# Attention scores of pairs 6 and 7 from two products of rounded operands in place of one float32 product, in a fused attention and feed-forward kernel with a written-out issue order

## The chip, the core and the metric

The kernel runs on one core of a Trainium2 chip. The metric is the device time of one execution in microseconds (us). Five engines work side by side: TensorE (PE, with its weight loads shown apart as PEld), VectorE (DVE), ScalarE (ACT), GpSimd (POOL) and the queue of SyncE (SP), from which nearly all DMAs are issued in order. A difference of 0.3%, some 3.1 us here, is about what a measurement of this kernel can tell from no change.

## What is computed

```
q, k, v: 8 batches x 8 heads x 576 x 64 float32;  f: 8 x 8 x 576
scores = q k^T / 8 + cum[i] - cum[j],  cum = cumsum(log(clip(f)));  causal
attn   = softmax(scores);   x = attn v            (4608 tokens x 512)
h = x w_in (512 x 2048);    out = (h cos h) w_out  (2048 x 512)
```

## The kernel before, in words

**Units.** The attention is cut into 32 pairs of heads (pair n belongs to batch n // 4), the feed-forward part into 16 units of tokens (unit u is one half of a batch, 320 or 256 tokens). A pair has two heads. Per head the causal scores are made in three groups of row blocks, one PSUM tile each: block 4 (two products of 288 columns), blocks 3 and 0 (448 and 64 columns), blocks 2 and 1 (320 and 192 columns). After a product, DVE adds the mask and finds the row extreme (line 879, 705 for pairs 0 to 3), ACT makes exp and the row sum (884, 715), POOL and DVE the reciprocal of the sum (889, 892), and ACT and DVE write the normalized weights as a high and a low float16 half (901, 905); a DMA transposes them (910) and PE multiplies them with v (934).

**Three kinds of scores.** `N32` and `NQ` set which pairs take which way. Pairs below `N32` = 4 are float32 throughout (`attention32`, scores in line 697, transposes on PE in line 668). Pairs from `N32` up to `NQ` = 8 load q and k as float32 (`load32`: one 288 KB load in line 636 and two loads of one row of the running sum in line 640 per head) and make the scores in one float32 product of 66 rows (line 865; the trace has each as two records). Pairs from `NQ` on run `prep` per head: a 576 KB load of q and k, laid out twice over 128 partitions (line 800), one rounding of all 1152 columns (line 801 on ACT or 802 on POOL), a DMA that copies rounded rows from tile to tile (803), two loads of rows of the running sum (806), and two subtractions that leave the rest after rounding (808 and 809, each on DVE or POOL). Their scores are two products of rounded operands that add up in PSUM (lines 867 and 868).

**Shared tiles.** The four q/k tiles of the float32 pairs are taken over by the two sets of the rounded pairs. At pair `NQ` an operation on POOL (`make`, line 787) clears each set (lines 369 to 371 and 791); it may start when the float32 pairs are done with those two tiles.

**The issue order.** Every operation is recorded with its engine and what it reads and writes, and `ORDER`, a table of numbers, says in which order the operations are issued; each engine runs its own in that order. A letter `a` behind a number takes the other engine (POOL for a rounding, a subtraction or a split). `+m` puts m filler products in front of a PE operation (line 1077: a constant tile times a constant mask of 448 columns, into the tile that the operation is about to overwrite). They compute nothing that is used.

```
N32, NQ, NACT = 4, 8, 1                                             # 44
gens = [(attention32 if n < N32 else attention)(n) ...]
if n < NQ: xb, q32 = load32(n, hd)                                  # attention
else: prep(hd); xb, q32 = list(SB[sets[hd]].values()), None
if q32: T.matmul(c, q32[0:66, 0, isl], q32[0:66, 1, d], ...)        # 865
else:                                                               # 867, 868
    T.matmul(c, hi[:, 0, isl], hi[:, 1, d], start=True, stop=False)
    T.matmul(c, co[0:68, 0, isl], co[0:68, 1, d], start=False, stop=True)
for _ in range(pads): T.matmul(fill(), ones, mask[:, 0:PAD], ...)   # 1077
```

The feed-forward part is `gemm1` (lines 964 to 994) and `gemm2` (1010 to 1019), with twelve float16 products to an operation. The weights are read as 64-bit words, converted, bounded and split at the start (lines 483 to 519), beside the pairs of batch 0.

Of the kernel before, what the change touches and what calls it, by code (L numbers as in the profile page):

```python
# [43 lines left out]
N32, NQ, NACT = 4, 8, 1  # L44
# [8 lines left out]
0 50 60 55 70 25 1 2 4 51 27 52 26 72 61 71 53 62 54 63 3 65 11 56 192 57 95 64 100 6 58 125 7a 170 33+44 28 34 35 40+1 66 37 29 36 67 12  # L53
85+1 41 59 68 78+1 30 175 86 124 96 69 73+1 191 87 42 9 79 44 123 31+1 97 185 38+2 155 215 80 101 156 245 157 74 190 158+3 39 98 81 13 171
32 159 43 176 172 45+2 177 10 48 160 178 75 161 15 311 173 82 131+6 312 162 102 47 163 88 126+1 89 186 46 132 116 138+1 149 174 187 164 180
127 83 24 93 150 216 84 139 179 205+4 133 140 49 217 430 135 243 188 14 90+8 218 1439 16 206 244 94 110 17 207 18 76+1 134 165 19a 92 181
198 128 117 182 91 20 193 199 189 183 141 425 115 166 21 431 200 184 167 77 435 432 142 310 275 22 219 433 276 5 23 146 277a 194 251+1 147
# [14 lines left out]
796 586a 786 601 604 813 787 597 797 818 542 799 617 605 798 819 602 773 598 800 820 618+1 801 607 814 802 606 949 821 619 803 948 825 804  # L72
620 774 621 599 822 837 805 622 826 623 608 624 806 658 600 625 807 641 662+1 827 626 828 838 659 642 808 678 627 839 643 609 676+1 823 628
679 644 663 629 664+2 809 677 630 645 810 829 631 646 811 830 660 840 831 632 832 610 672 665 661 633 841 877+1 634 673 647 674+1 878 635
648a 824 833 611 834 858+3 933 836 842 636 714 879 843 637 859 649 692 638 844 835 650 675 845 639 698 612 893 651 984 860 640 865 652 693
666 880 861 862 667 613 699 653 846 614 668 694 654 700 847 848 655 669 863 889 657 670 680 681 715 986 710 947 656 682 864 695 881 866 1438
701 867 683 868 882 869 696 883 895 870 671a 871 884 697 885 926 712 872 886 873 887 684 874 849 1148 890 876 875 896 702 902 853 891 927
914 897 903 850 716 898 711 1022 851 945 904 915 713 899 726 916 905 888 717 906 718 917 730 727 907 728 731 985 908 918 719 1026 900 919
1029 854a 969 909 703 920 901 729 724 910 921 911 922 720 913 912 950 970 923 686 685a 951 924 971 972 957 1027a 704 958 925 959 952 721 687
973 953 725 954 974 1031 960 955 975 732 1021 994 961 928 956 962 1082 963 733 964 965 976 987 966 977 734 995 1083 968 1032 978 705 996 967  # L80
979 997 735 941 929 1006 998 980 1445 999 688 1007 1023 1008 1000 988 1009 689 1010 1229 989 1028 1001 706 690 1011 990 1002 1012 691 991
1013 1003 1030 1014 946 1273 722 707 1015 992 723a 1004 1016 942 981 993 1017 736 934 943 737 1230a 1084 982 708 983 709 1085 1234a 1231
1033 1005 1018 1034 935 936a 1235 1040 1019 1086 1020 1052 1041 937 1068 1274a 1053 938 1054 1042 1055 1278a 1275 1070 1035 1276 1956 1043
1232 1036 1037 1069 939 1072 940 1056 1038 1071 1044 1074 1073 1045 1446 1046 1024 1057 1058 1279 1124 1314 1075 1047 1277 1076 1233 1270
1077 1126 1125 1048 1059 1039 1078 1122 1957 1025 1064 1049 1127 1060 1120 1061 1065 1050 1079 1243 1121 1062 1123 1236 1271 1128 1140 1080
1066 1129 1255 1100 1318 1315 1081 1051 1130 1134 1320a 1237 1238 1131 1101 1102 1244 1132 1087 1239 1319a 1256 1317 1245 1240 1103 1063
1257 1141 1246 1133a 1241 1287 1258 1138 1242 1259 1316 1288 1104 1247 1289 1280 1248 1290 1260 1249 1136 1250 1281 1135 1251 1291 1252 1139
# [1020 lines left out]
```

## Time and profile before

| | |
|---|---|
| Runs | 1042.11, 1043.04, 1045.21 us; median 1043.04 |
| The profiled execution's own time | 1040.97 us |
| Its span, first to last instruction | 1039.0 us |
| Busy, share of the span | PE 99%, PEld 80%, DVE 75%, ACT 76%, POOL 28% |
| Granted TensorE clock over the span | 1.00 of full speed |
| DMA | 144.77 MB, mean 139 GB/s |

The profiled execution stands 2.07 us under the median of the runs, and 1.97 us of its own time lie outside the span. PE's busy time counts a matmul from its start to its modelled end, so neighbours overlap; what one costs the engine is the distance from its start to the start of what follows.

### The profile page before, as it was taken

The numbers are of one execution on the slowest core, as the hardware profiler recorded it, in microseconds if no ns is written. First come the engines' busy times: TensorE is split into PE (matmuls) and PEld (weight loads), VectorE is DVE, ScalarE is ACT, GpSimd is POOL, SyncE is SP. The second block draws the span as 40 slices with busy tenths as digits, with TensorE's granted clock in tenths as the row PEclk, the third lists the DMA queues.
The fourth block names the chain that finished last, engine by engine and source line by source line (L and its number), as shares of the span: only waits on it lengthen the run. The fifth ranks groups of instructions, "written<-read, shape, count | busy, mean of one in ns | idle before, by whom it ended". The sixth has DMA issues, their size and how long they took to land. (4 is left out here: it accounts for less than half of the span.)

```text
span 1039.0 us, 23384 instructions
## 1 busy us (share of the span) xinstructions
PE 1027.0 (99%) x8915; PEld 831.6 (80%) x8916; DVE 774.9 (75%) x1710; ACT 789.5 (76%) x1711; POOL 294.8 (28%) x381
## 2 busy tenths in 40 slices
PE   8999999999999999999999999999999999999998
PEld 4788777778888877888778877888778877888787
DVE  8999998778678676787877688586877967663531
ACT  5999999788768797898877789686878877753431
POOL 3223213432341343332332424233141313300110
PEclk9999999999999999999999999999999999999999
DMA  8997525856685757668465766947466583520001
GB/s 261 288 321 200 130 55 128 185 107 162 154 175 147 163 132 163 139 144 183 114 145 135 176 142 159 193 83 164 124 170 136 121 189 56 122 39 16 7 14 34
DMA packets 255920, 144.77 MB, mean 139 GB/s; under 512 B 223736, under 2 KB 231928, under 8 KB 255808
## 3 DMA queue, kind: packets, MB, share of 16 engines
q1 hardware_dynamic: 255680, 143.27, 58.4%
q8 instruction: 70, 1.15, 0.4%
q14 instruction: 42, 0.34, 0.1%
q10 hardware_dynamic: 128, 0.01, 0.0%
HBM read 71.41 MB, written 9.68 MB: 78 GB/s over the span
## 5 line engine op out<-in xcount | busy, mean ns | idle before, releaser
L1010 PE MATMUL hp<-g,W2s 128*128 128x320 f16 (+1 forms) x3072 | 391.8, 286 | 0.2
L964 PE MATMUL hp<-xh,W1s 128*128 128x320 f16 (+1 forms) x2048 | 381.3, 286 | 1.5 <-ACT h L970 1.4
L964 PEld LDWEIGHTS <-W1s 128*128 128x128 f16 x3072 | 295.5, 98 | 78.6 <-issue 1.8
L1010 PEld LDWEIGHTS <-W2s 128*128 128x128 f16 x3072 | 296.3, 98 | 76.1 <-issue 0.6
L964 PE MATMUL hp<-xl,W1s 128*128 128x256 f16 (+1 forms) x1024 | 292.6, 286 | 0.0
L905 DVE SCALAR_TENSOR_TENSOR PS<-pa,ri,PS 128x576 f16<-128x576 f32 (+3 forms) x280 | 146.1, 544 | 57.3 <-ACT PS L901 55.9
L884 ACT ACTIVATE pa<-pa,nb 128x576 f32<-128x576 f32 (+4 forms) x280 | 141.5, 506 | 48.5 <-DVE nb L879 43.1
L901 ACT ACTIVATE PS<-pa,ri 128x576 f16<-128x576 f32 (+3 forms) x280 | 137.7, 531 | 31.1 <-DVE ri L892 27.0
L889 POOL TENSOR_SCALAR ri<-L 128x1 f32<-128x1 f32 (+1 forms) x168 | 53.9, 321 | 352.0 <-ACT pa L884 347.1
L879 DVE CUSTOM_DVE_ANT_0 pa<-pa,mask 128x576 f32<-128x576 f32 (+4 forms) x280 | 134.7, 500 | 24.0 <-PE pa L868 20.4
L970 ACT ACTIVATE h<-hp 128x320 f32<-128x320 f32 (+1 forms) x256 | 100.1, 411 | 36.5 <-PE hp L964 32.8
L994 POOL TENSOR_TENSOR g<-h,g 128x1024 f16<-128x1024 f32 (+1 forms) x32 | 83.5, 2609 | 149.0 <-ACT g L992 147.3
L985 DVE TENSOR_TENSOR h<-h,r 128x1280 f32<-128x1280 f32 (+1 forms) x64 | 89.6, 1399 | 34.4 <-ACT r L983 33.9
L983 ACT ACTIVATE r<-r,halfpi,m_inv 128x1280 f32<-128x1280 f32 (+1 forms) x64 | 86.2, 1348 | 31.2 <-DVE r L981 29.0
L981 DVE SCALAR_TENSOR_TENSOR r<-r,m_b,h 128x1280 f32<-128x1280 int32 (+1 forms) x64 | 93.6, 1462 | 1.1
L867 PE MATMUL pa<-Q 128*128 128x288 f32 (+4 forms) x288 | 90.4, 327 | 1.2 <-DVE PS L905 0.7
L979 DVE TENSOR_SCALAR r<-h,m_a 128x1280 int32<-128x1280 f32 (+1 forms) x64 | 54.9, 858 | 44.9 <-ACT h L970 43.0
L992 ACT CAST g<-h 128x1280 f16<-128x1280 f32 (+1 forms) x64 | 73.8, 1154 | 10.6 <-DVE h L985 10.4
L934 PEld LDWEIGHTS <-vv 128*64 128x64 f16 x1512 | 68.6, 110 | 10.3 <-issue 9.5
L868 PE MATMUL pa<-Q 68*128 68x288 f32 (+4 forms) x288 | 76.6, 304 | 0.0
L934 PE MATMUL pa<-pt,vv 128*64 128x256 f16 (+2 forms) x1512 | 76.6, 254 | 0.0
L1016 ACT ACTIVATE ot<-hp,m_o 128x320 f32<-128x320 f32 (+1 forms) x64 | 32.2, 503 | 47.6 <-PE hp L1010 36.2
(127 smaller groups left out, 1182.5 us busy)
## 6 DMA issues: line engine op xcount, KB each, us to landing
stage<-in_dram SPq DMA_DIRECT2D x48, 576.0 KB
stage<-in_dram SPq DMA_DIRECT2D x32, 320.0 KB
v<-in_dram SPq DMA_DIRECT2D x32, 320.0 KB
h<-in_dram SPq DMA_DIRECT2D x16, 512.0 KB
g<-in_dram SPq DMA_DIRECT2D x16, 512.0 KB
Q<-Q SPq DMA_DIRECT2D x48, 144.0 KB
out_dram<-ot SPq DMA_DIRECT2D x32, 160.0 KB
Q<-in_dram SPq DMA_DIRECT2D x16, 288.0 KB
```

Source lines behind the costliest of these rows:

```text
L867: T.matmul(c, hi[:, 0, isl], hi[:, 1, d], start=True, stop=False)
L879: op("DVE", c_dve(w) + 0.008, lambda view=view, ib=ib, o=o, w=w, mk=mk, c=c: V.tensor_tensor_reduce(out=view(ib, o, w), in0=view(ib, o, w) ...
L884: op("ACT", c_act(w, True, 2), lambda view=view, ib=ib, o=o, w=w, c=c: A.activation(view(ib, o, w), view(ib, o, w), AF.Exp, bias=nb.get()[ ...
L901: op("ACT", c_act(w, True, 1), lambda view=view, ib=ib, o=o, w=w, c=c, out_=out_: A.activation(out_(0), view(ib, o, w), AF.Copy, scale=ri. ...
L905: op("DVE", c_dve(w) + 0.06, lambda view=view, ib=ib, o=o, w=w, c=c, out_=out_: V.scalar_tensor_tensor(out_(1), view(ib, o, w), ri.get()[: ...
L934: T.matmul(d, vv.get()[:, jb, hd, kv], m, start=first and x == 0, stop=last and x == 2)
L964: T.matmul(hp.get()[:, 0:w_], WS_[1][:, at(1, 4 * c + cb), w, fs], x.get(), start=(n == 0), stop=(n == 11))
L970: op("ACT", c_act(w_, True), lambda hp=hp, k=k: A.activation(h.get()[:, k, 0:w_], hp.get()[:, 0:w_], AF.Copy, scale=float(2.0 ** -24)), re ...
L981: op("DVE", c_dve(N) + 0.045, lambda: V.scalar_tensor_tensor(fl(r), fl(r).bitcast(I32), b1.get()[:, c:c + 1], fl(h), op0=ALU.mult, op1=ALU ...
L983: op("ACT", c_act(N, aps=2), lambda: A.activation(fl(r), fl(r), AF.Sin, scale=inv.get()[:, c:c + 1], bias=halfpi), reads=[inv], writes=[r] ...
L985: op("DVE", c_dve(N), lambda: V.tensor_tensor(fl(h), fl(h), fl(r), op=ALU.mult), reads=[r], writes=hk, prio=pr)
L1010: T.matmul(po.get()[:, 0:w_], WS_[2][:, at(2, 4 * c + k), w, msl], gh.get()[:, i, k, 0:w_], start=(n == 0), stop=(n == 47))
```

## The change

One constant changes, `NQ` from 8 to 6, and the whole of `ORDER` (4,299 operations before, 4,315 after).

```diff
-N32, NQ, NACT = 4, 8, 1
+N32, NQ, NACT = 4, 6, 1
 ...
 ORDER = """
-0 50 60 55 70 25 1 2 4 51 27 52 26 72 61 71 53 62 54 63 3 65 11 56 192 57 95 64 100 6 58 125 7a 170 33+44 28 34 35 40+1 66 37 29 36 67 12
 ...
```

The table's rows tell a reader nothing; what it does is counted from the two tables. Pairs 6 and 7 go over from `load32` to `prep`. Filler products: 44 in front of the first score product before, 36 now; behind it 55 before, 83 now. Of these 55 and 83 lie 39 and 56 in front of PE operations of pairs 0 to 3 or of the scaling of the weights and of v, 16 and 27 further on. The four roundings of pairs 6 and 7 are one on POOL and three on ACT, their eight subtractions five on DVE and three on POOL. Over the whole program ACT has 9 roundings more and POOL 5 fewer, DVE 2 subtractions fewer and POOL 10 more. POOL has 2 fewer of the splits of the weights and 2 fewer of v, DVE as many more. The number of changes between the exp and the sine tables on ACT is the same.

PE at the start of the program; `pa` and `hp` are PSUM tiles, PS the staging tile of the softmax, L1077 a filler. Before, the rows behind the 44 fillers:

```order
L697 MATMUL pa_166<-Q 128x448
L697 MATMUL pa_166<-Q 128x64
L697 MATMUL pa_213<-Q 128x288 x2
L1077 LDWEIGHTS ones
L1077 MATMUL pa_219<-mask,ones 128x448
L697 MATMUL pa_219<-Q 128x320
L697 MATMUL pa_219<-Q 128x192
L1077 LDWEIGHTS ones
L1077 MATMUL pa_231<-mask,ones 128x448
L697 MATMUL pa_231<-Q 128x320
L697 MATMUL pa_231<-Q 128x192
```

Of the change, behind its 36 fillers:

```order
L697 MATMUL pa_160<-Q 128x448
L697 MATMUL pa_160<-Q 128x64
L697 MATMUL pa_202<-Q 128x288 x2
L697 MATMUL pa_209<-Q 128x320
L697 MATMUL pa_209<-Q 128x192
L1077 LDWEIGHTS ones
L1077 MATMUL pa_218<-mask,ones 128x448
L697 MATMUL pa_218<-Q 128x320
L697 MATMUL pa_218<-Q 128x192
L668 MATMUL hp<-eyef,PS_81 128x128 x4
```

The first head's three groups now stand together, behind eight fillers fewer, and the first transposes follow the second head's first group.

PE at the first score group of pair 6 (L964 is `gemm1` of unit 1). Before:

```order
L964 MATMUL hp<-xl_1637,W1s 128x256
L1077 LDWEIGHTS ones
L1077 MATMUL pa_1858<-mask,ones 128x448
L865 MATMUL pa_1858<-Q 128x320
L865 MATMUL pa_1858<-Q 128x192
L1077 LDWEIGHTS ones
L1077 MATMUL hp<-mask,ones 128x448
L964 LDWEIGHTS W1s
```

Now:

```order
L964 MATMUL hp<-xl_1578,W1s 128x256
L867 MATMUL pa_1893<-Q 128x320
L868 MATMUL pa_1893<-Q 128x320
L867 MATMUL pa_1893<-Q 128x192
L868 MATMUL pa_1893<-Q 128x192
L1077 LDWEIGHTS ones
L1077 MATMUL hp<-mask,ones 128x448
```

Two float32 products became four of rounded operands, and both fillers stand behind the group.

The SP queue at the operands of pair 6 (v, Q, stage: the loads of v, the q/k tiles, the loads of q and k and of v; pt: transposed softmax weights). Before:

```order
L640 DMA Q<-cum_d 1x576
L636 DMA Q<-in_dram 64x2x576
L910 DMA_TRANSPOSE pt_2024<-PS_82 128x12x128
L640 DMA Q<-cum_d 1x576
L636 DMA Q<-in_dram 64x2x576
L1019 DMA out_dram<-ot 128x320
```

Now:

```order
L910 DMA_TRANSPOSE pt_1520<-PS_82 128x12x128
L803 DMA Q<-Q 64x576
L910 DMA_TRANSPOSE pt_1718<-PS_81 128x18x128
L806 DMA Q<-cum_d 2x576
L582 DMA stage<-in_dram 128x640
L806 DMA Q<-cum_d 2x576
L800 DMA stage<-in_dram 128x1152
```

The copy of the rounded rows and the two row loads of pair 6's first head stand between transposes, where a load from memory and one-row loads stood.

## Rows read from the trace of the kernel before

**Rows 1.** The page: busy time of each engine, its share of the span and its instructions; and the granted TensorE clock in 40 equal slices of the span, in tenths (9 is 0.9 or more).
```profile
PE 1027.0 (99%) x8915; PEld 831.6 (80%) x8916; DVE 774.9 (75%) x1710; ACT 789.5 (76%) x1711; POOL 294.8 (28%) x381
...
PEclk9999999999999999999999999999999999999999
```

**Rows 2.** The table of windows: from and to in us of the span, length, busy time of each engine (with its instructions), granted clock, DMA share and GB/s.
```profile
0.00:13.00 13.00, 10.71 (x45) 5.22 (x46) 9.80 (x17) 4.79 (x8) 6.42 (x24) 1.00 0.74 224
13.00:60.00 47.00, 44.27 (x278) 34.21 (x277) 44.64 (x129) 39.83 (x119) 10.51 (x20) 1.00 0.97 292
60.00:100.00 40.00, 39.62 (x290) 34.20 (x289) 39.42 (x120) 38.24 (x112) 12.36 (x28) 1.00 0.87 258
100.00:143.00 43.00, 42.65 (x344) 32.28 (x343) 42.04 (x92) 40.79 (x89) 7.98 (x13) 1.00 0.46 105
143.00:206.00 63.00, 62.58 (x529) 48.29 (x529) 52.95 (x118) 55.48 (x113) 22.84 (x32) 1.00 0.62 141
206.00:1039.00 833.00, 827.20 (x7442) 677.41 (x7436) 586.01 (x1240) 610.38 (x1274) 234.69 (x267) 1.00 0.56 125
```

**Rows 3.** The same windows for the fillers of line 1077 alone: length, PE and PEld with their counts.
```profile
13.00:60.00 47.00, 10.32 (x39) 3.93 (x39) 1.00 0.97 292
...
206.00:1039.00 833.00, 0.00 (x0) 0.00 (x0) 1.00 0.56 125
```

**Rows 4.** The chain of work that ended last, in order of time: start in us, us, engine, tile, line, how many.
```profile
951.61 19.91 PE hp L964 x156
...
1001.59 34.01 PE hp L1010 x288
```

**Rows 5.** The waits of PE over the whole span, longest first: who waited for whom, us in total, times, longest.
```profile
PE pa L1077 <- POOL ones L346: 2.3, 1, 2.3
PE hp L964 <- ACT h L970: 1.4, 3, 0.6
PE hp L668 <- ACT PS L715: 1.1, 1, 1.1
```

**Rows 6.** The timeline of PE: the float32 score groups of pairs 6 and 7 (one row each, four records) and the row that follows each.
```profile
166.27 1.14 PE L865 MATMUL pa<-Q 66*128 66x288 f32 x4
167.24 0.38 PE L964 MATMUL hp<-xh,W1s 128*128 128x256 f16 x2
...
176.95 1.03 PE L865 MATMUL pa<-Q 66*128 66x320 f32 x4
177.81 0.38 PE L964 MATMUL hp<-xh,W1s 128*128 128x256 f16 x2
...
181.73 1.08 PE L865 MATMUL pa<-Q 66*128 66x448 f32 x4
182.65 1.52 PE L1010 MATMUL hp<-g,W2s 128*128 128x320 f16 x10
```

**Rows 7.** The timeline of PE: score groups of pair 8, made from rounded operands (the first row of each and the row that follows the group; the first two lines are the costliest group found at its start).
```profile
204.92 0.38 PE L867 MATMUL pa<-Q 128*128 128x288 f32 x1
...
205.64 1.11 PE L934 MATMUL pa<-pt,vv 128*64 128x64 f16 x24
...
222.62 0.47 PE L867 MATMUL pa<-Q 128*128 128x448 f32 x1
...
223.27 0.38 PE L867 MATMUL pa<-Q 128*128 128x288 f32 x1
...
223.90 0.45 PE L964 MATMUL hp<-xh,W1s 128*128 128x320 f16 x2
...
225.44 0.41 PE L867 MATMUL pa<-Q 128*128 128x320 f32 x1
...
226.04 1.16 PE L1010 MATMUL hp<-g,W2s 128*128 128x256 f16 x9
```

**Rows 8.** The timeline of PE: the fillers at the start and the first score products, and a run of eight fillers later with the row that follows it.
```profile
2.29 10.56 PE L1077 MATMUL pa<-mask,ones 128*128 128x448 bf16 x44 [2.29 <-POOL ones L346]
...
12.69 2.11 PE L697 MATMUL pa<-Q 66*128 66x448 f32 x8
...
32.01 1.68 PE L1077 MATMUL hp<-mask,ones 128*128 128x448 bf16 x8
33.52 0.60 PE L668 MATMUL hp<-eyef,PS 128*128 128x128 f32 x4
```

**Rows 9.** Groups of instructions by line: line, engine, operation, out<-in, count, then busy us, mean ns, and idle time before them.
```profile
L809 POOL TENSOR_TENSOR Q<-stage,Q 64x576 fp32r<-64x576 f32 x25 | 40.2, 1608 | 30.3 <-ACT Q L801 28.7
...
L802 POOL CAST Q<-stage 128x1152 fp32r<-128x1152 f32 x25 | 31.5, 1259 | 75.2 <-PE pa L867 44.3 <-DMA stage<-in_dram 16.3 <-DVE nb L879 6.4
L808 DVE TENSOR_TENSOR Q<-stage,Q 64x576 fp32r<-64x576 f32 x33 | 27.9, 847 | 4.7 <-ACT Q L801 2.4 <-POOL Q L802 1.4
...
L801 ACT CAST Q<-stage 128x1152 fp32r<-128x1152 f32 x23 | 26.5, 1153 | 4.2 <-PE pa L867 3.2 <-POOL ri L889 0.6 <-issue 0.3
```

**Rows 10.** One line's instructions: duration in ns at the least, median and most.
```profile
L808 DVE TENSOR_TENSOR Q<-stage,Q x33: 754/755/1920, 185.2 to 878.4; 64x576 fp32r<-64x576 f32 x33
```

**Rows 11.** The timeline of POOL and of the SP queue at the operands of pair 8's first head: the rounding, transposes, the copy of rounded rows, the last row load.
```profile
181.75 1.14 POOL L802 CAST Q<-stage 128x1152 fp32r<-128x1152 f32 x1
...
189.43 5.76 SPq L910 DMA_TRANSPOSE pt<-PS  x2
...
195.87 0.57 SPq L803 DMA_DIRECT2D Q<-Q  x1
...
198.67 0.62 SPq L806 DMA_DIRECT2D Q<-cum_d  x1
```

More of the change, by code (lines that the diff above doesn't have):

```diff
@@ L72 @@
[L72 to L75, printed above, removed]
@@ new lines @@
+969 1046 976 1047a 989 1045 977 970 978 703 688 979 990 980 991 722 982 981 1005 992 1006 734 723a 993 1013 1024 951 1025 939 1007 1098 956
+994 1014 944 1026 689 1015 1008 1009 1048 1016 1027 1017 707 1018 1044 735 1028 1245 690 1029 945 1019 691 1030 1286 1099 1020 1031 1021
+1032 1100 736 1033 1022 1034 946 1035 995 737 708 1010 947 1101 1246 1011 709 948 1289 952 1049 996 1023 1050 1036+3 997 1051 953 1068 1037
+1102 1056 1038 949 1084 1057 1290 1251 1058 1069 1086 1059 1295a 1039 1070 1060 1248 1085 1249 1071 1061 1052 1088 1247 950 1072 1053 1294
@@ new lines @@
+1514 1573 1554 1238 1555 1585 1568 1239 1605 1810 1803 1764 1574 1807 1603 1569 1240 1215 1812a 1601 1586 1604 1575 1570 1216 1606 1571
+1811a 1576 1607 1241 1572 1776 1587 1769 1974 1639 1202 1770 1602 1556 1608 1971 1588 1808 1809 1777 1627 1847 1242 1577 1628 1589 1578 1579
+1771 1609 1580 1633 1772 1610 1640 1243 1629 1778 1581 1244a 1779 1582 1611 1634 1975 1584 1583 1773 1788 1590 1591 1621 1848a 1780 1630
+1853 1852a 1592 1932 1622 1851 1593 1631 1594 1781 1595 1623 1789 1596 1790 1782 1612 1791 1635 1774 1792 1775 1615 1783 1793 1850 1613 1891
@@ new lines @@
+1724 2028 2492 2050 2041 2051 2284a 2052 1720 2060 1727 2285 2053 2042 1748 1695a 1725 2282 1721 2043 2073 2044 2281 1722 2061 2045 2283
+1749 2054 2062 2055 2083 1723 2063 1750 2057 2084 1728 2085 1734 2064 1729 2065 2086 2066 1751 1738 1735 2067 1730 2068 2056 1740 2087 2069
+1736 1741 1731 1739 1752 1737 2323 1732 1742 1981 1743 2088 1754 1982 1744 2089 2070 1983 1733 1984 1755 2286 2074 2114 2287 1753 2071 2288
+2072 1745 2122 2075 1746 2090 1756 2102 2115 2091 1747a 2321 2124 2326 2103 2324 2104 2092 2116 1757 2093 2118 2325 2328a 2364 2125 2123
@@ new lines @@
+2731 2921 2950 2949 2973 2963 2959 2974 2721 2723 2960 2975 2961 2736 3011 2672 2712 3066 3023 2962 2976 2980 2737 2981 2713 2724 2982 2977
+2725 2992 2983 2732 2978 2714 2964 3070 2984 3107 3067 2985 3027 2742 3024 2726 3068 3072a 3009 2743 2993 3110 2979 3071a 3012 2965 2733
+2986 2994 2987 3013 3014a 2988 2995 2989 3032 2727 2991 3039 2744 2734 3033 2996 2990 3040 2997 3051 2998 2999 2745 3000 3111a 3034 3001
+3052 3069 3041 3035 3053 2735 2738 3116a 3042 3002 3036 3115 3003 3037 2739 3054 3043 3044 3045 2748 3112 3038 3046 3313 2740 2741 2749 3047
@@ new lines @@
+3246a 3265 3494 3252 3498 3584 3479 3511 3499 3500 3589 3480 3495 3588a 3501 3496 3512 3627 3266 3513 3587 3257 3544 3530 3502 3586 3531
+3514 3515 3546 3503 3267 3516 3830 3517 3258 3504 3518 3505 3440 3268 3506 3519 3508 3441 3556 3507 3549 3568 3550 3259 3628 3557 3558 3569
+3551 3273 3520 3481 3552 3559 3560 3260 3561 3562 3553 3633 3554 3585 3570 3563 3261 3555 3629 3571 3631 3482 3572 3573 3564 3262 3574 3632
+3575 3576 3565 3566 3590 3577 3263 3536 3264 3591 3567 3578 3609 3537 3592 3538 3597 3610 3580 3831a 3611 3598 3269 3274 3612 3836 3835a
@@ new lines @@
+3954 3754 3955 3733 3743 3970 3764 3992 3744 3734a 3971 3993 3751 3972 3973 3745 3765 3994 4047 3995 3957 3974 3776 3975 3746 3976 4045a
+4007 4014 3747 4008 3997 4015 3755 3977 4016 3978 4049a 3979 3766 3980 3981 3998 3982 4017 3748a 3777 3984 3983 4009 3999 4026 3752 4027
+4086a 4050 3767 3753 4090a 4018 3996 4028 3778 3768 4042 4010 4019 4011 3758 4012 3779 3769 3759 4029 4046 4087 4013 4089 3782 4048 4020
+3958 4088 4021 4022 4030 4023 3783 3760 4031 4025 4024 4032 4070 4058 4033 4051 4034 3784 3780 4035 3761 3785 4071 3762 4036 4052 4037 3763
@@ L201 @@
+4166 4167 4233 4225 4234 4226 4235 4236 4277 4227 4228 4283 4229 4278 4230 4279 4281 4280 4284 4255 4282 4285 4263 4286 4256 4253 4287 4264
+4249 4288 4243 4289 4271 4272 4250 4290a 4254 4244 4273 4245 4274 4246 4257 4258 4237 4259 4238 4275 4260 4297 4261 4247 4239 4262a 4248
+4240 4276a 4298 4241 4242 4291 4292 4299 4303 4304 4300 4293 4301 4302 4305 4294 4306 4295 4296 4309 4310 4307 4308 4311 4312 4313 4314
 """
```

228 lines of the change are left out of this document (107 added, 121 removed), and 36 rows, old and new, of the table ORDER.

## The prediction, as it was put on record before the run

> **What bounds the kernel now.** I read the busy line first: PE 99%, DVE 75%, ACT 76%, the clock full throughout [rows 1]. That is an average over stages, so the table of windows comes next [rows 2]. It shows two regimes. From 13 to 143 us, while the weights are prepared beside the first pairs, DVE is busy 44.64 of 47, 39.42 of 40 and 42.04 of 43 us, ACT 39.83, 38.24 and 40.79. PE looks just as full there, but of its 44.27 us from 13 to 60, 10.32 are 39 fillers that compute nothing used [rows 3]. In this stage DVE and ACT set the pace and PE is padded. From 206 us to the end there is no filler [rows 3], PE is busy 827.20 of 833 us, and DVE and ACT only 586 and 610 [rows 2]. The chain that ends last is PE alone for long stretches: its last 288 products, of 320 or 256 columns, take 34.01 us, 0.118 each [rows 4]; at the granted clock of 1.00 [rows 1], the 2.4 GHz level, 256 columns are 0.107 us and 320 are 0.133. Between the two, from 143 to 206 us, lie the scores of pairs 6 and 7; DVE has 10 us free there and ACT 7.5. The list of PE's waits shows that little is left to gain by removing waits: 2.3 us before the first filler, then 1.4 and 1.1 [rows 5].
>
> So the time is this: all that PE issues, fillers included, by its spacing, plus what it idles in the first 143 us. That idle time is 47 - 44.27 = 2.7 us up to 60 us, then 0.4 and 0.35 [rows 2]. A PE microsecond saved behind 143 us is a microsecond of the end; one saved before it is worth something only if DVE and ACT keep up.
>
> **The score products.** Each of four heads exchanges three float32 groups for three groups of rounded operands. By the start of a group and of what follows it, float32 costs 167.24 - 166.27 = 0.97 us, 0.86 and 0.92, in all 2.75 us a head [rows 6]. The rounded kind costs 223.27 - 222.62 = 0.65, then 0.63, and 0.60, in all 1.88 [rows 7]. That is 0.87 us a head, 3.5 us for four. The dearest first group is 0.72 [rows 7], which leaves 0.78 a head, 3.1 us, as the lower bound. In the trace of before these products stand where PE is the pace, or just behind: -3.5 us.
>
> The busy share alone would mislead here. The Trainium skill ("Perfetto Trace Analysis", section Identifying the Most-Contended Engine) says that matmul busy time is no measure of PE's headroom and that the share of weight loads is. By that rule PE stands at 80% [rows 1], the 3.5 us would be swallowed by slack, and the sum below would end 3.5 us higher. The spacing of 0.118 us [rows 4], which is what the columns take, disagrees for the stage that counts: there is no slack between products.
>
> **The fillers.** Eight fillers in a row last 33.52 - 32.01 = 1.51 us, 0.189 each [rows 8]. At the start 36 stand in place of 44: the first score product can start 8 x 0.189 = 1.5 us earlier, if q, k and the rows of the running sum are there. Before, PE did not wait behind the last filler [rows 8], so how much earlier they land isn't seen: -1.5 us, bounds -1.5 and 0. I take the early end because in the new SP order only one load of q and k stands ahead of these rows, not two. Then 56 fillers in place of 39 in the first pairs: 17 x 0.189 = +3.2 us. Further on 27 in place of 16: +2.1 us. These 5.3 us count fully only where PE would not have idled. PE idled 2.7 us from 13 to 60 us [rows 2]; fillers that fall into such a gap cost nothing. The bounds are 0 and all 3.5 us of idle time to 143 us; I take half of the first gap, -1.4 us, since DVE's own work up to that point is the same.
>
> **The new operands.** The price per head is one rounding, 1.15 us on ACT or 1.26 on POOL, and two subtractions, 0.85 us on DVE, or up to 1.61 on POOL [rows 9]. Three roundings on ACT are 3.5 us, five subtractions on DVE 4.2 us. Most fall behind 143 us, where both engines have room [rows 2]; I cost them at nothing. Only pair 6's first head falls into the crowded stage: two subtractions, 1.7 us, where DVE has 1.0 us free of 43. That cover is thin; the rival below prices its loss. On the SP queue each head adds a copy and a larger load and takes away nothing but a smaller load; its transposes are waited for in the queue, two of them held it 5.76 us [rows 11]. Pair 8 shows the chain before: rounding at 181.75, copy at 195.87, last row load at 198.67, product at 204.92 [rows 7, 11], so 6.2 us from the last load to the product, and PE did not wait. In the new order the PE work between the same two points of pair 6, by these durations, is four operations of twelve products, at 0.118 to 0.128 us a product [rows 4], and five fillers, 6.6 to 7.1 us. I take no wait. Clearing the shared tiles moves forward by two pairs, with the same instructions: nothing.
>
> **The sum.** -3.5 - 1.5 + 3.2 + 2.1 - 1.4 = -1.1 us, so 1039.9 us against the profiled execution's own 1040.97. That one stands 2.07 us under the median of the runs; carried over, 1041.9 us against 1043.04. With every bound on the good side: -3.5 - 1.5 + 5.3 - 3.5 = -3.2, 1039.8. On the bad side: -3.1 + 0 + 5.3 - 0 = +2.2, 1045.2. That is the likeliest case's own range, nearly all of it within 0.3% (3.1 us), about what a measurement can tell from no change.
>
> **Rival 1, slower: DVE runs over before pair 6.** In its fullest stretch DVE has 1.0 us free [rows 2] and gets subtractions for pairs 6 and 7 that were not there. If its queue decides until the scores of pair 7, the five on DVE push PE back by 5 x 0.85 = 4.2 us, and the extra fillers absorb nothing: -3.5 - 1.5 + 5.3 + 4.2 = +4.5, 1047.5 us. It decides from the point where DVE is over 98% busy up to pair 6's first product. The same subtraction has taken 754 ns and 1920 ns [rows 10], so something stretches it. For it: 42.04 of 43. Against: 10 us of room right behind. The Trainium skill ("SBUF — State Buffer", section Terms) says that DVE and GpSimd share a port pair that one of them holds alone, so that the loser stands still; the trace's 1920 ns fits that, and the roundings and subtractions that go to POOL would then cost DVE too, which is this rival. Chance 0.13.
>
> **Rival 2, faster: the fillers cost nothing.** If DVE and ACT set the end of the first stage whatever PE issues, the 17 fillers only replace idling: -3.5 - 1.5 + 2.1 = -2.9; if the later eleven do so too, -5.0. That gives 1038.0 to 1040.1, middle 1039.0 us. For it: DVE's 94 to 99% [rows 2]. Against: PE was itself busy 126.5 of 130 us there, so there are only 3.5 us to replace. Chance 0.27, of which 0.02 for its upper edge, within 0.3%.
>
> **Rival 3, slower: the new order waits where the old did not.** From 206 us PE has 833 us without a filler [rows 3] and its waits for ACT over the whole span are 1.4 us in three and one of 1.1 [rows 5]. All of that part is reordered. Four new waits like that one of 1.1 us would make -1.1 + 4.4 = +3.3, 1046.3 us. Nothing in the trace speaks for it but that the order is new. Chance 0.09.
>
> **Rival 4: the products are no cheaper.** The issue order shows the rounded kind in place, so it would have to cost as much as float32: +2.4, 1045.4 us. Rows 7 speak against it. Chance 0.03.
>
> **The numbers.** The forecast has 0.48. Faster by over 0.3% is rival 2 without its edge: 0.25. Slower by over 0.3% are rivals 1 and 3: 0.22. Within 0.3% are the forecast, rival 4 and that edge: 0.48 + 0.03 + 0.02 = 0.53. The range is 1038.8 to 1047.0: from just under the middle of rival 2 to just under rival 1, which leaves out some 0.1 at either end.
>
> **What would show it.** Right: three groups of pair 6 with lines 867 and 868 at 0.60 to 0.72 us each; first score product near 11.2 us of the span; PE busy 98% or more from 143 us on. Wrong: PE idle for over 2 us just ahead of line 867's first row (rival 1), idle in 13 to 60 us falling to nothing with that stage no longer than before (rival 2), or waits of PE behind 206 us that add up to more than 3 us (rival 3).

## The result and the profile after

The change made the kernel slower: median 1047.44 us (20 runs, 1044.63 to 1060.12) against 1042.64 us of the kernel before beside it, ratio 1.0052, 95% interval 1.0034 to 1.0069. I had forecast 1041.9 us and a range of 1038.8 to 1047.0. The profiled execution took 1050.83 us, its span is 1048.8 us.

The busy line and the granted clock, which answer to [rows 1]:
```profile
PE 1031.9 (98%) x8936; PEld 836.8 (80%) x8936; DVE 777.0 (74%) x1714; ACT 798.8 (76%) x1720; POOL 285.9 (27%) x376
...
PEclk8999999999999999999999999999999999999999
```
The averages hardly moved, but one slice of the clock did. The windows, as in [rows 2], and those of the fillers alone, as in [rows 3]:
```profile
0.00:13.00 13.00, 9.78 (x41) 4.67 (x42) 9.87 (x18) 4.90 (x8) 5.28 (x23) 1.00 0.56 157
13.00:60.00 47.00, 44.74 (x240) 33.45 (x240) 38.94 (x113) 33.62 (x99) 9.02 (x18) 0.85 0.88 279
60.00:100.00 40.00, 38.55 (x279) 33.85 (x279) 38.93 (x117) 38.14 (x112) 11.54 (x26) 1.00 0.88 284
100.00:143.00 43.00, 42.25 (x332) 31.78 (x331) 42.34 (x94) 37.77 (x82) 8.26 (x18) 1.00 0.52 113
143.00:206.00 63.00, 58.89 (x501) 46.50 (x500) 57.20 (x120) 61.18 (x123) 22.84 (x26) 1.00 0.60 125
206.00:1039.00 833.00, 831.15 (x7493) 680.98 (x7491) 589.75 (x1257) 621.75 (x1297) 228.97 (x266) 1.00 0.57 128
```
```profile
13.00:60.00 47.00, 15.69 (x53) 6.03 (x53) 0.85 0.88 279
...
206.00:1039.00 833.00, 0.74 (x3) 0.21 (x3) 1.00 0.57 128
```
Two stretches went wrong. From 13 to 60 us the clock averages 0.85. From 143 to 206 us PE is idle 63 - 58.89 = 4.1 us, where it was idle 0.4 before; ACT stands at 61.18 of 63 us (before 55.48), DVE at 57.20 (before 52.95). Behind 206 us PE is busy 831.15 of 833 us. The windows stand at fixed times, and the change starts its first product of `gemm1` at 105.41 us, against 96.65 before, so the two don't hold quite the same work. The stretch S of the experiments does.

The start, in the timeline of PE (as [rows 8]), and the window in which the clock was down:
```profile
9.70 1.30 PE L1077 MATMUL pa<-mask,ones 128*128 128x448 bf16 x6
11.93 3.05 PE L697 MATMUL pa<-Q 66*128 66x448 f32 x12 [0.93 <-DMA Q<-vv]
...
16.40 2.05 PE L697 MATMUL pa<-Q 66*128 66x320 f32 x4 [1.24 <-DMA Q<-in_dram]
...
30.12 1.03 PE L697 MATMUL pa<-Q 66*128 66x320 f32 x4
```
```profile
16.00:30.00 14.00, 13.60 (x42) 9.17 (x43) 7.42 (x24) 6.62 (x24) 1.21 (x2) 0.51 0.80 253
```
The first score product starts at 11.93 us, not at 12.69; it had to wait 0.93 us for a row of the running sum, and the second head's first product 1.24 us for its q and k. From about 16 us on the granted clock is at 0.5, the 1.2 GHz level, for some 14 us: the same four records take 2.05 us at 16.40 and 1.03 at 30.12.

The score groups, as [rows 6, 7], and the lines of the operands, as [rows 9]:
```profile
176.50 0.40 PE L867 MATMUL pa<-Q 128*128 128x288 f32 x1
...
177.19 1.80 PE L1010 MATMUL hp<-g,W2s 128*128 128x320 f16 x12
...
181.28 0.47 PE L867 MATMUL pa<-Q 128*128 128x448 f32 x1
...
181.93 0.39 PE L867 MATMUL pa<-Q 128*128 128x320 f32 x1
...
182.52 0.40 PE L964 MATMUL hp<-xh,W1s 128*128 128x256 f16 x2
```
```profile
L801 ACT CAST Q<-stage 128x1152 fp32r<-128x1152 f32 x32 | 36.8, 1150 | 8.9 <-PE pa L867 5.9 <-DMA stage<-in_dram 3.1
L802 POOL CAST Q<-stage 128x1152 fp32r<-128x1152 f32 x20 | 24.1, 1207 | 30.5 <-PE pa L867 19.1 <-PE pa L868 4.9 <-DMA stage<-in_dram 3.7
```
A head now costs 0.69 + 0.65 + 0.59 = 1.93 us of PE in place of 2.75: the products are as cheap as forecast, 3.3 us for four heads. ACT has 32 roundings in place of 23, nine more over the whole program. The prediction priced only the three of pairs 6 and 7; two of the others are pair 8's.

Whom PE waited for from 100 to 206 us, longest first (as [rows 5]):
```profile
PE hp L964 <- ACT h L970: 1.0, 1, 1.0
PE pa L865 <- PE pa L934: 0.8, 1, 0.8
PE pa L934 <- DVE PS L905: 0.7, 1, 0.7
PE hp L1077 <- ACT h L970: 0.6, 1, 0.6
PE pa L867 <- DVE PS L905: 0.6, 1, 0.6
```
None is longer than 1.0 us. Most of them wait for evictions and softmax work of ACT and DVE, none for the new operands themselves. The signs that I had named came out so: score groups at 0.59 to 0.69 us (right), the first product at 11.93 us and not near 11.2, PE busy 93% and not 98% from 143 to 206 us (wrong), and no idle time of 2 us just ahead of line 867's first row (against rival 1).

### The profile page after: what moved, and what is told of

The parts are those of the page before. It is cut to its first block, busy times and chain, and to the rows that moved or that the text cites. A ratio compares the mean times of both kernels' runs of the same rounds, so it can differ in the third digit from the quotient of the medians.

```text
span 1048.8 us, 23437 instructions
## 1 busy us (share of the span) xinstructions
PE 1031.9 (98%) x8936; PEld 836.8 (80%) x8936; DVE 777.0 (74%) x1714; ACT 798.8 (76%) x1720; POOL 285.9 (27%) x376
## 4 chain that ended last, share of the span: by engine, by line
PE 56%; ACT 3%; DVE 2%; issue 1%; DMA 1%; POOL 0%; ACTq 0%
PE hp L1010 24%; PE hp L964 23%; PE pa L934 4%; PE pa L867 3%; PE pa L868 2%; ACT pa L884 1%; DMA out_dram<-ot 1%; ACT PS L901 0%; DVE PS L905 0%; ACT g L992 0%; ACT L983 0%; ACT L884 0%; DVE pa L879 0%; ACT r L983 0%; ACT h L970 0%
## 5 line engine op out<-in xcount | busy, mean ns | idle before, releaser
L964 PE MATMUL hp<-xh,W1s 128*128 128x320 f16 (+1 forms) x2048 | 381.4, 286 | 1.4 <-ACT h L970 1.4
L964 PEld LDWEIGHTS <-W1s 128*128 128x128 f16 x3072 | 295.6, 98 | 80.5 <-issue 3.0
L964 PE MATMUL hp<-xl,W1s 128*128 128x320 f16 (+1 forms) x1024 | 292.8, 286 | 0.0
L905 DVE SCALAR_TENSOR_TENSOR PS<-pa,ri,PS 128x576 f16<-128x576 f32 (+2 forms) x280 | 145.6, 545 | 55.1 <-ACT PS L901 54.1
L901 ACT ACTIVATE PS<-pa,ri 128x576 f16<-128x576 f32 (+2 forms) x280 | 138.8, 530 | 32.8 <-DVE ri L892 21.1
L970 ACT ACTIVATE h<-hp 128x256 f32<-128x256 f32 (+1 forms) x256 | 99.0, 409 | 34.6 <-PE hp L964 32.7
L994 POOL TENSOR_TENSOR g<-h,g 128x1024 f16<-128x1024 f32 (+1 forms) x32 | 80.7, 2523 | 158.3 <-ACT g L992 141.8
L867 PE MATMUL pa<-Q 128*128 128x288 f32 (+4 forms) x312 | 97.1, 326 | 1.9 <-DVE xl L942 1.0
L868 PE MATMUL pa<-Q 68*128 68x288 f32 (+4 forms) x312 | 82.9, 304 | 0.0
```

The costliest lines, as they stand in the source:

```text
L901: op("ACT", c_act(w, True, 1), lambda view=view, ib=ib, o=o, w=w, c=c, out_=out_: A.activation(out_(0), view(ib, o, w), AF.Copy, scale=ri. ...
L905: op("DVE", c_dve(w) + 0.06, lambda view=view, ib=ib, o=o, w=w, c=c, out_=out_: V.scalar_tensor_tensor(out_(1), view(ib, o, w), ri.get()[: ...
L964: T.matmul(hp.get()[:, 0:w_], WS_[1][:, at(1, 4 * c + cb), w, fs], x.get(), start=(n == 0), stop=(n == 11))
L970: op("ACT", c_act(w_, True), lambda hp=hp, k=k: A.activation(h.get()[:, k, 0:w_], hp.get()[:, 0:w_], AF.Copy, scale=float(2.0 ** -24)), re ...
```

## The experiments

The times scatter by more than the effects, in part since the granted clock falls for some microseconds in part of the runs, of the kernel before too. So the table gives, beside the ratio, the number of runs whose mean clock was under 0.9985 and the median of the others, "at full clock". **Idle** is PE's idle time from 100 to 206 us of the profile. **S** is the stretch from the first score block of pair 5 to the first of pair 9; it is the same work in the same order in all kernels with the change's order, and in two more profiles in which only the start differs it is 137.6 and 138.4 us, so 1 us of S is noise. Kernels 7, 8, 9 and 11 ran beside runs of the kernel before whose median at full clock is 1041.4 us; beside the other experiments it is 1042.0 to 1042.3.

| | ratio, 95% interval | clock fell | at full clock, us | idle, us | S, us |
|---|---|---|---|---|---|
| before (110 runs beside these kernels) | 1 | 19 of 110 | 1042.1 | 0.8 | other order |
| the change | 1.0052, 1.0034 to 1.0069 | 9 of 20 | 1046.7 | 4.9 | 137.3 |
| 1 order alone | 1.0012, 0.9981 to 1.0043 | 5 of 12 | 1044.6 | 2.1 | 137.2 |
| 2 float32 product on the new operands | 1.0063, 1.0041 to 1.0086 | 7 of 12 | 1047.6 | 3.5 | 139.3 |
| 3 scores in the old order | 1.0054, 1.0024 to 1.0083 | 9 of 12 | 1050.0 | 11.4 | other order |
| 4 the same, placed earlier | 1.0079, 1.0047 to 1.0110 | 6 of 8 | 1051.8 | 10.1 | other order |
| 5 pair 7 alone, old order | 1.0063, 1.0038 to 1.0088 | 5 of 9 | 1046.7 | 4.4 | other order |
| 6 roundings on POOL | 1.0018, 0.9988 to 1.0048 | 5 of 12 | 1046.0 | 6.0 | 138.6 |
| 7 subtractions on POOL | 1.0084, 1.0058 to 1.0109 | 3 of 5 | 1048.5 | 8.3 | 141.3 |
| 8 short subtractions | 1.0052, 1.0026 to 1.0077 | 4 of 10 | 1045.0 | 5.2 | 137.7 |
| 9 short roundings | 1.0045, 1.0027 to 1.0064 | 4 of 8 | 1045.2 | 4.4 | 136.8 |
| 10 both short | 1.0032, 1.0009 to 1.0054 | 6 of 12 | 1045.4 | 4.6 | 137.7 |
| 11 28 fillers fewer | 1.0119, 1.0056 to 1.0181 | 4 of 4 | none | 4.9 | 136.5 |
| 12 13 late fillers fewer | 1.0038, 1.0016 to 1.0061 | 6 of 12 | 1046.1 | 6.1 | 137.9 |
| 13 before with 36 fillers at the start | 1.0006, 0.9980 to 1.0031 | 6 of 12 | 1040.9 | 0.7 | other order |
| 14 load early and 44 fillers | 1.0036, 1.0006 to 1.0067 | 2 of 12 | 1047.6 | 5.1 | 138.4 |
| 15 44 fillers | 1.0044, 1.0021 to 1.0067 | 5 of 12 | 1044.7 | 4.5 | 137.6 |

**1. The order alone.**
```diff
-N32, NQ, NACT = 4, 6, 1     # order and fillers of the change;
+N32, NQ, NACT = 4, 8, 1     # the operand work of pairs 6 and 7 is left out of ORDER
```


> The change's issue order and its 28 extra filler products, with the scores of pairs 6 and 7 left in float32 (no roundings, subtractions, copies or extra rows for them; pair 8's roundings on ACT as in the change). Theory T (the loss of about 4.8 us against the kernel before has two causes: the start, where the order issues the q/k load of the second head late and has 8 fillers fewer, and 130 to 206 us, where the operand work of pairs 6 and 7 makes PE wait for full ACT and DVE): no waits of the second kind, but 3.7 us of score work back; the 28 fillers +3.8, the start +1 at full clock (more in runs in which the clock falls at 16 us): 1047 us, ratio about 1.004, and PE without holes over 0.3 us for ACT h or DVE between 130 and 206 us beyond those of the kernel before. Rival O (the order itself, and not the operand work, makes PE wait there): 1050 to 1051 us, ratio 1.008, the same holes as in the change. Rival F (fillers lie in idle time): 1043.5 us.

At full clock it took 1044.6 us, nearest to rival F. Rival O fell: PE's idle time is 2.1 us, not the 4.9 of the change.

**2. A float32 product on the new operands.**
```diff
+    if n < 8:
+        T.matmul(c, hi[0:66, 0, isl].bitcast(F32), hi[0:66, 1, d].bitcast(F32), start=True, stop=True)
+        continue
     T.matmul(c, hi[:, 0, isl], hi[:, 1, d], start=True, stop=False)
```


> The change with all operand work of pairs 6 and 7 kept, in its places, but each of their score blocks made by one float32 product of 66 rows of the rounded q and k in place of two rounded products (decay sums and rounding errors are left out of these scores). On PE this is the price of the kernel before, 3.7 us more than the change. Theory X (from 130 to 206 us ACT and DVE are the bound, so what PE saves there comes back as waits): PE's lost time up to 206 us falls by 3 us or more, time as the change within 1 us: 1046.5 us at full clock, ratio 1.004 to 1.005. Theory W (PE's waits there are for late operands and have nothing to do with how long the scores take): 3.7 us slower than the change, 1050 us, ratio 1.008.

With the change these two make a staircase of one step each. S is the distance of the first two rows of PE's timeline below, the third row is the last twelve products of the program (the lines are 870 and 1013 in the second kernel); first for the order alone, then with the operand work, then for the change:
```profile
110.37 0.65 PE L865 MATMUL pa<-Q 66*128 66x288 f32 x2
...
247.62 0.41 PE L867 MATMUL pa<-Q 128*128 128x320 f32 x1
...
1039.30 1.47 PE L1010 MATMUL hp<-g,W2s 128*128 128x256 f16 x12
```
```profile
109.68 0.65 PE L865 MATMUL pa<-Q 66*128 66x288 f32 x2
...
249.01 0.41 PE L870 MATMUL pa<-Q 128*128 128x320 f32 x1
...
1040.77 1.47 PE L1013 MATMUL hp<-g,W2s 128*128 128x256 f16 x12
```
```profile
116.31 0.89 PE L865 MATMUL pa<-Q 66*128 66x288 f32 x3
...
253.63 0.41 PE L867 MATMUL pa<-Q 128*128 128x320 f32 x1
...
1044.08 1.47 PE L1010 MATMUL hp<-g,W2s 128*128 128x256 f16 x12
```
So the operand work lengthens the stretch by 139.3 - 137.2 = 2.1 us, twice its noise, and the cheaper products take 139.3 - 137.3 = 2.0 us off it again, not 3.3.

The end of S is not the end of the program. From pair 5's first row to the last twelve products the three take 928.9, 931.1 and 927.8 us, and kernels 14 and 15, the same work as the change, 928.6 and 928.1; 0.8 us is the noise of this. So up to the end the operand work costs 2.2 us, and the cheaper products give back 2.5 to 3.3: what was missing in S came behind it.

The medians at full clock say +3.0 and -0.9. They include the start. Kernel 2 and the change are the same program up to the scores of pair 6, and the first row of pair 5 stands at 109.68 us in kernel 2, at 110.37 in kernel 1 and at 108.27 in kernel 6, all at a clock of 1.00. No profile of the change itself held the clock, so what its start takes then is not seen. By these profiles medians of four to eleven runs don't settle 2 us.

Of the three kernels' PE windows from 100 to 206 us the idle time is what grows:
```profile
100.00:206.00 106.00, 103.92 (x827) 78.29 (x825) 94.76 (x206) 98.34 (x204) 26.09 (x41) 1.00 0.52 111
```
```profile
100.00:206.00 106.00, 102.55 (x810) 76.54 (x808) 97.29 (x208) 99.76 (x204) 29.43 (x45) 1.00 0.56 118
```
```profile
100.00:206.00 106.00, 101.14 (x831) 78.28 (x830) 99.53 (x213) 98.95 (x204) 31.10 (x44) 1.00 0.56 120
```
That is 2.1, 3.5 and 4.9 us. Theory X wanted no difference between 2 and the change, theory W 3.7 us. In S both hold in part; up to the end the 2.5 to 3.3 us are nearer to W.

**3, 4, 5. The scores in the old order**: all operand work put by hand into the order of before, then put earlier, then for pair 7 alone.
```diff
-N32, NQ, NACT = 4, 8, 1
+N32, NQ, NACT = 4, 6, 1     # 5: 4, 7, 1; ORDER and fillers as before, and in it, per head:
+857 858 859 860 861 862 863   # load, rounding, copy, two row loads, two subtractions (pair 6, first head),
                               # each at a place of its own
```


> The kernel before's issue order and fillers with the rounded scores of pairs 6 and 7 put into it: for each head the load, the rounding on ACT (the first of pair 6 on ACT too), the copy of q, two row loads, two subtractions (three of eight on POOL), at the places at which the change has them. Theory T: the scores give 3.7 us on PE, and the operand work on ACT and DVE takes 3 to 4.5 of it back as waits between 130 and 206 us; start and clock as before: 1042 to 1043.5 us, ratio 0.999 to 1.001. Rival O (the order alone is at fault, the operand work is hidden): 1039 us, ratio 0.9965. Rival P (rounded products gain less on PE than 3.7 us): 1045 us or more, with the score products of pairs 6 and 7 over 11.5 us a pair.

> The kernel before's order with the rounded scores of both pairs, as in the earlier run of that kind, but with the operand work placed earlier: three of four roundings on POOL, 40 or more places ahead of the products, the last head's subtractions on DVE. Theory P (that run's 13.9 us of lost time came from the placement by hand: an ACT that stood 1.4 us for a load and scale factors that stood behind POOL's subtractions): lost time between 120 and 206 us falls to 6 us or less, 1042 to 1043.5 us, ratio 0.9995 to 1.001. Theory X (the order of the kernel before leaves no room for this work wherever it is put): 8 us or more lost, 1045 us or more, ratio 1.003 or more.

> The kernel before's order and fillers with the scores of pair 7 alone from rounded operands (pair 6 stays float32; the float32 tiles are numbered the other way round so that the first head's rounded tiles are free after pair 5). One rounding on POOL, one on ACT, the four subtractions on DVE, set 20 or more places ahead of the products that use them. My prediction's step (the operand work hides in the room that ACT and DVE have behind 143 us): half of the score gain, 1.8 us faster: 1040.5 us, ratio 0.998. Theory X (PE's gain there turns into waits for ACT and DVE, and the operand work adds to both): no difference or up to 2 us slower, ratio 1.000 to 1.002.

All three are slower than the change or equal to it, so the old order does not take the work in where I put it. Kernel 3, at 1050.0 us, is slower than its theories T and O allowed; its time would fit rival P, but the products are as cheap as in the change, so PE's 11.4 us of idle time make the difference. Theory P of 4 fell: placed earlier, PE was still idle 10.1 us. Kernel 5 lost more than both of its theories allowed. In kernel 3 the timeline of POOL and DVE shows one way in which it hurts:
```profile
188.83 2.38 POOL L809 TENSOR_TENSOR Q<-stage,Q 64x576 fp32r<-64x576 f32 x1
...
191.16 1.14 POOL L802 CAST Q<-stage 128x1152 fp32r<-128x1152 f32 x1
...
192.38 0.46 POOL L889 TENSOR_SCALAR ri<-L 128x1 f32<-128x1 f32 x2
192.61 0.17 DVE L892 RECIPROCAL ri<-ri 128x1 f32<-128x1 f32 x1 [2.65 <-POOL ri L889]
```
The softmax's scale factor, half a microsecond of work, stood behind a subtraction and a rounding in POOL's queue, and DVE stood 2.65 us behind it. PE's own longest wait there, 2.2 us, was for that subtraction.

**6, 7. The operand work on POOL.**
```diff
-899 ... 958 ... 999 ... 1043 ... 1246           # 6: roundings
+899a ... 958a ... 999a ... 1043a ... 1246a
-863 ... 862 ... 903 ... 904 ... 962             # 7: subtractions
+863a ... 862a ... 903a ... 904a ... 962a
```


> The change with five roundings moved from ACT to POOL: pair 6's second head, both heads of pair 7, both of pair 8 (ACT 1.15 us each; POOL 1.64 us where the trace of before shows it). Theory T (PE waits between 130 and 206 us because ACT and DVE are full): ACT has 5.8 us less to do, the holes for ACT h shrink: 2 us faster than the change, about 1045.4 us, ratio 1.003. Rival V (DVE alone is the late one, and POOL's roundings hold it up more): no gain or up to 1.5 us slower than the change, ratio 1.005 to 1.007.

> The change with the five subtractions of pairs 6 and 7 that DVE makes moved to POOL, in the same places of the order. Theory D (DVE is the late one of 120 to 206 us; moving roundings off ACT gained nothing there): DVE has 3.8 us less, PE's lost time between the first product of pair 5 and 206 us falls from 6.9 us to about 4, and the kernel is 2 to 3 us faster than the change at the same start: 1044 us, ratio 1.0015. Rival Q (POOL's subtraction takes 1.4 us in place of 0.75 and stands ahead of the scale factors of the softmax on POOL, which DVE then waits for): lost time unchanged or more, ratio 1.004.

Theory T of 6 fell: with 5.8 us taken off ACT, S did not shrink. Theory D of 7 fell: S grew by 4 us, as rival Q had it.

**8, 9, 10. Short operand work.**
```diff
-  ... e.tensor_tensor(hi[up, 0, ks], qk.get()[up, 0], ...             # 8: pairs 6, 7; S = 576
+  ws = 8 if n < N32 + 4 else S
+  kw_ = slice(64, 64 + ws)
+  ... e.tensor_tensor(hi[up, 0, kw_], qk.get()[up, 0, 0:ws], ...
-  ... A.copy(hi[:, :, ks], qk.get()) ...                              # 9: pairs 7, 8
+  wc = 8 if n in (7, 8) else S                                        # 10: also pair 6's second head
+  kc = slice(64, 64 + wc)
+  ... A.copy(hi[:, :, kc], qk.get()[:, :, 0:wc]) ...
```
Kernels 8 and 10 also clear, once and on POOL, columns that nothing else writes then.


> The change with the eight subtractions of pairs 6 and 7 made on 8 columns in place of 576 (the rounding errors of q and k are left out of their scores), every instruction in its place. This takes 5 x 0.7 us from DVE and 3 x 1.3 us from POOL. Theory D (DVE is late, its subtractions are what the change costs there): lost time of PE between pair 5's products and 206 us falls from 6.9 us to 3.5, that of the change's order alone: 1043.5 us, ratio 1.001. Rival A (ACT's roundings are the cost): 6 us lost still, 1046.5 us, ratio 1.004.

> The change with the roundings of pairs 7 and 8 made on 8 columns in place of 576 of each of q and k (their scores are then those of older operands), every instruction in its place. This takes 4 x 1.1 us from ACT between 165 and 215 us. Theory D (DVE is late): lost time of PE up to 206 us falls by less than 1 us, 1046.5 us, ratio 1.004. Rival A (ACT's roundings are the cost): it falls by 2 to 3 us, 1044.5 us, ratio 1.002; the waits for ACT h after pair 6 go.

> The change with the subtractions of pairs 6 and 7 and the roundings of pair 6's second head and of pairs 7 and 8 all made on 8 columns in place of 576 (rounding errors and most of q and k are left out of these scores), every instruction in its place: 5 x 0.7 us less on DVE, 5 x 1.1 us less on ACT, 3 x 1.3 us less on POOL. Each of the two alone changed PE's lost time by under 1 us. Theory X (ACT and DVE wait for each other in the softmax chains, both must be relieved): lost time between 120 and 206 us falls from 6.9 us to 3 to 4 us, 1043.5 to 1044.5 us with the same start, ratio 1.0015 to 1.0025. Rival O (the waits come from the order and from the landing of the loads, not from the work): still 6 us, 1046.5 us, ratio 1.004.

S is 137.7, 136.8 and 137.7 us against 137.3: how long the roundings and subtractions last does not decide. Up to the end kernel 10 takes 928.0 us, the change 927.8. Theory D of 8, rival A of 9 and theory X of 10 fell. At full clock the three are 1.3 to 1.7 us faster than the change, but beside 8 and 9 the kernel before was 0.7 us faster too; with four to six runs each I don't count that as shown. What is left of the 2.1 us is that these steps exist: their places in five in-order queues and what they wait for. This is what remains; no run of its own shows it. The SP queue of the change shows such a place:
```profile
154.73 14.18 SPq L910 DMA_TRANSPOSE pt<-PS  x3
169.00 2.48 SPq L806 DMA_DIRECT2D Q<-cum_d  x4
171.58 0.53 SPq L803 DMA_DIRECT2D Q<-Q  x1
```
Three transposes, with their waits, hold it 14.18 us, and rows and copies of the next heads stand behind them. Which queue makes the 2.1 us I have not separated.

**11, 12. Fewer fillers.**
```diff
-73+6 ... 138+4 ... 131+9 ... 1036+3             # 11: 28 of the later fillers out (four of twelve places)
+73+1 ... 138+2 ... 131+5 ... 1036
-664+4 ... 660+3 ... 678+1 ... 674+2 ... 714+2 ... 1036+3     # 12: 13 between 150 and 215 us out
+664+1 ... 660+1 ... 678   ... 674   ... 714   ... 1036
```


> The change with 28 of its later filler products left out, 21 of them in pairs 0 and 1 and the others about pairs 5 to 7; the 36 ahead of the first product stay. Theory T (a filler costs its whole 0.19 us where PE doesn't wait): 28 x 0.19 = 5.3 us; about 3 us of it comes back as waits that the fillers had stood in, so 2 to 3 us faster than the change, 1044.5 us, ratio 1.002. Rival F (fillers lie in waits only): no difference, 1047 us, with PE's waits longer by 5 us. Rival C (the clock needs them): the granted clock falls in more runs, 1050 us or more.

> The change with 13 of its filler products between 150 and 215 us left out (those of pairs 0 to 5 and of the start stay). Theory X (PE waits for ACT and DVE there in any case, the fillers stand in waits): no difference from the change, 1046.5 us at full clock, PE's lost time 2.5 us more. Theory T (a filler costs its 0.19 us): 2.5 us faster, 1044 us, ratio 1.0015. Rival C (the clock needs these fillers): granted clock under 1.0 between 100 and 206 us, 1049 us or more.

In 11 the clock fell in all four runs, in the profile twice (0.91 up to 100 us, 0.90 behind):
```profile
0.00:100.00 100.00, 89.78 (x516) 69.78 (x516) 86.05 (x240) 74.28 (x213) 24.74 (x62) 0.91 0.88 258
100.00:206.00 106.00, 101.15 (x746) 78.93 (x746) 91.71 (x192) 88.93 (x187) 26.27 (x44) 0.90 0.51 108
```
Rival C of that run was right. In 12 PE's idle time from 100 to 206 us rose from 4.9 to 6.1 us, within S from 5.2 to 7.5, and S and the time stayed: the 13 x 0.19 = 2.5 us of these fillers stand in waits. What the early ones cost is not shown, since without them the clock fell in every run.

**13, 14, 15. The start.**
```diff
-33+44
+33+36                                           # 13, in the kernel before
-0 50 60 25 55 1 2 3 4 51 5 ... 53 70 62 ... 33+36
+0 50 60 25 55 70 1 2 3 4 51 5 ... 53 62 ... 33+44   # 14, in the change; 15: 33+44 alone
```


> The kernel before with 36 fillers ahead of the first score product in place of 44, and nothing else changed. By my prediction's term the first product starts 1.5 us earlier: 1041.1 us, ratio 0.9985. Theory S (the product then waits for q and k, and the DMA-bound first 60 us take back what is left): no difference, 1042.5 us, with a wait of PE of about 1 us at 11 to 12 us. Rival C (the clock falls after that wait, as in the profile of the change): a granted clock of 0.99 in several runs, and 1045 us or more in these.

> The change with its start mended: the q/k load of pair 0's second head goes right behind the first loads, ahead of the copy of the decay sums, and 44 fillers stand ahead of the first score product in place of 36. Theory T: no wait of PE for q or k in the first 20 us, granted clock full in every run: about 1046 us, ratio 1.0035, and no run over 1048; the later holes stay. Rival C (the clock's fall has another cause than the waits at 12 and 15 us): the clock still falls at about 16 us in some runs, and the median stays at 1047.4, ratio 1.005. Rival D (the second load, issued early, delays the first head's): PE's first product after 13 us and 1048 us.

> The change with 44 fillers ahead of the first score product in place of 36, the loads where the change has them. If the 8 fillers alone decide over the clock's fall: it falls in 2 or fewer of 12 runs (9 of 20 in the change), median 1047 us, ratio 1.004, and no run at full clock under 1045. If the late load of the second head's q and k makes the clock fall: it falls in 4 or more of 12, median 1048 us.

In 13 the eight fillers are worth 1042.1 - 1040.9 = 1.2 us while the clock holds, and the clock falls in 6 of 12 runs, which then take 1046.2 us in the median; of the 35 runs of the kernel before beside it, it fell in 3. Its profile is of the second kind. PE waited 0.60 us, its first product starts at 12.71 us, no earlier than the 12.69 of before, and the clock was down from about 38 to 50 us:
```profile
12.71 1.46 PE L697 MATMUL pa<-Q 66*128 66x448 f32 x5 [0.60 <-DMA Q<-vv]
```
```profile
38.00:50.00 12.00, 12.00 (x56) 10.12 (x55) 9.17 (x25) 6.42 (x19) 2.17 (x4) 0.57 0.80 247
```
14 lost the clock in 2 of 12 runs, 15 in 5 of 12; twelve runs don't tell these apart. 14, whose clock mostly held, is no faster than the change, but its first product comes only at 13.73 us, as its rival D had it. 15 is 2.0 us faster than the change at full clock, with its first product at 13.17 us. So neither the fillers alone nor the late load alone is shown to be the cause of the falls, and how much of the loss at full clock the start makes stays open.

## Why the prediction was wrong

**Right.** The products: 0.82 us a head cheaper where I had 0.87. The terms of start and fillers only as a sum: -1.5 + 3.2 + 2.1 - 1.4 = +2.4, and the order alone measured 1044.6 - 1042.1 = +2.5 us at full clock. That is luck, for the terms don't hold one by one: the eight fillers gave 1.2 us, the late fillers cost nothing (12), and what the early ones cost is not shown. From the first product of `gemm1` to the last product of all, the order alone takes 941.0 us, against 938.7 before and 938.0 in kernel 13, so waits of the new order, in which the late fillers stand, are a good part of the +2.5. Rival 3 did not happen: behind 206 us PE idles 1.9 us.

**The step that failed: "I cost them at nothing."** The operand work of pairs 6 and 7 cost 2.1 us in the stretch, 2.2 up to the end of the program, 3.0 in the medians at full clock (1 and 2). I had compared the work with the engines' free time, 10 us on DVE and 7.5 on ACT [rows 2]. That free time was no room for steps that must come at certain places of the queues: shortening them to nearly nothing left the stretch as it was (10). Which place or queue it was stays open. I had also counted, but not priced, the roundings that the order moves from POOL to ACT, whose room behind 143 us shrank from 7.5 to 1.8 us.

**The second, in doubt: "A PE microsecond saved behind 143 us is a microsecond of the end."** Of 3.3 us, 2.0 arrived within S and 2.5 to 3.3 up to the last products; the medians at full clock show 0.9, but they include the start. So this step is not shown to have failed, only to be late: PE was busy 62.58 of 63 us there [rows 2], and when its products got cheaper its idle time rose from 3.5 to 4.9 us (2 and the change), mostly in waits for steps of ACT and DVE. I had set the product spacing of [rows 4], which comes from 950 to 1036 us, against the rule of the Trainium skill ("Perfetto Trace Analysis", section Identifying the Most-Contended Engine) that matmul busy time is no measure of PE's headroom. Within S the runs lean to the rule, since 1.3 us of the 3.3 are missing there; up to the end they don't.

**The third, the start: "-1.5 us."** By the medians at full clock the fillers are worth 1.2 us (13), but no profile shows the way that I had in mind: the first product came at 12.71 us in kernel 13 and at 11.93 in the change, against 12.69, after a wait for a row of the running sum. It also left the clock out: in kernel 13 it fell in 6 of 12 runs, in the change in 9 of 20, in the kernel before in 19 of 110. In the change, 44 fillers did not mend that (15, 5 of 12). Its runs with a fall take 1050.8 us in the median, the others 1046.7; the median over all is 0.7 us higher for it.

**The sum as measured, at full clock:** 1042.1 + 2.5 (order and fillers) + 3.0 (operand work) - 0.9 (products) = 1046.7 us, and 1047.4 with the runs in which the clock fell. It comes out because each term is the difference of two neighbouring medians; it is no test. From pair 5 on, the profiles put operand work and products together at 927.8 to 928.6 against 928.9 us, so 0.3 to 1.1 us faster, where the medians say 2.1 us slower. Those 2.4 to 3.2 us lie ahead of pair 5, in the start, or are chance. From the first product of `gemm1` to the last product of all, the change takes 939.9 us and kernel 14 940.7, against 938.7 and 938.0: of the 4.6 us at full clock 1.2 to 2.7 are lost there. Where the rest is lost stays open. **Rival 1** gave 1047.5 us, but not for its reason: DVE is at 42.34 of 43 us before pair 6 as it says, yet how long its five subtractions last is not the price (8). No version beat the kernel before.

## What to carry to other kernels

That an engine is 99% busy does not show when a gain on it arrives; a run with the operation made dearer or cheaper and all else kept does (2), if it is read between two rows of the same work and up to the end of the program. Work that is "hidden" needs a place in its queue, so count what stands behind it there and what it waits for before costing it at nothing. With fewer fillers the clock fell more often (11 and 13), so give the chance of a fall, not only the price of the filler.

## What the runs showed of the hardware

The granted clock fell to half, the 1.2 GHz level, for 3 to 20 us at a time and came back. In every profile with a fall PE had waited about 1 us or more at one place not long before: 1.24 us in the change, 1.2 in kernel 8, 2.2 in kernel 5, and 1.2 in kernel 13, there some 7 us before. Not every such wait is followed by a fall: kernel 4 waited 2.8 us and kernel 3 2.2 us at a clock of 1.00. So the wait is not shown to be the cause. For one and the same program it differs from run to run: the change held the clock in 11 runs and lost it in 9. A subtraction on POOL took 1.40 us in the median and 2.38 us at 188.83 us of kernel 3, on DVE 0.75 in the median.
